# Three sets of small GpSimd loads beside a stream of large loads: attention over a cached window and a gated MLP for one token

## Chip, cores and metric

The kernel runs on one core of a Trainium2 chip. The metric is the device time of one execution in microseconds (us). The profile is of one execution on the chip, taken by the hardware profiler.

## What is computed

One token `x` (576 numbers, bfloat16) is normalised once and goes through two branches, whose results are added to `x`. Cut to what matters:

```python
def reference(A_x, A_k_cache, A_v_cache, A_wq, A_wo, B_x, B_w_in, B_w_sp, B_b_sp, B_w_out):
    def _A_ref(x, k_cache, v_cache, wq, wo):        # 32 query heads, 16 key heads of 128, window 4096
        q = (x @ wq).reshape(B, Sq, Hq, Dh) ...
        k = jnp.repeat(k_cache[:, :, Sk - W:, :], rep, axis=1)
        v = jnp.repeat(v_cache[:, :, Sk - W:, :], rep, axis=1)
        scores = jnp.einsum('bhqd,bhkd->bhqk', q, k) * Dh ** (-0.5)
        o = jnp.einsum('bhqk,bhkd->bhqd', _softmax(scores), v)
        return o... @ wo
    def _B_ref(x, w_in, w_sp, b_sp, w_out):
        z = _gelu(jnp.einsum('bsd,df->bsf', x, w_in))
        z1, z2 = z[..., :Fh], _layernorm(z[..., Fh:])
        g = jnp.einsum('ts,bsf->btf', w_sp, z2) + b_sp[None, :, None]
        return jnp.einsum('bsf,fd->bsd', z1 * g, w_out)
    xn = _layernorm(A_x)
    return A_x + _A_ref(xn, A_k_cache, A_v_cache, A_wq, A_wo) + _B_ref(xn, B_w_in, B_w_sp, B_b_sp, B_w_out)
```

The keys and values of the window are 16 heads x 4,096 positions x 128 numbers each; together with the weights 51 MB are read.

## The kernel before

The 16 key heads are worked on in four batches `b` of four. For each batch, `turn(b)` transposes the keys on VectorE in eight pieces (L209), `scores(b)` multiplies them with the query on TensorE (L254) and makes the softmax's exponentials (ScalarE, L274), and `values(b)` multiplies these with the values (L288) and sums up (L296). The calls stand in the order turn 0, scores 0, turn 1, scores 1, values 0, turn 2, scores 2, values 1, turn 3, scores 3, then `z_all` (the product with `w_in`, L311) and `gate` of the MLP branch, then values 2 and 3. At the end `row_of` (L376) adds the products with `wo` and `w_out` into one row, which is stored in two halves (L390 on SyncE, L391 on ScalarE). The schedule is manual: each engine runs its instructions in the order in which they are written, and a framework puts in the waits.

All large loads are issued by SyncE, in this order: `wq` in two cuts, k0, k1, v0, k2, v1, k3, `win`, v2, v3, `wo` in two cuts, `wout` in four (helpers `load`, L92, and `load_kv`, L98). Each has 128 rows, one for each partition. The tiles come from two pools of two buffers each, so a load waits until its buffer is free. In the pool `large` (20,736 numbers per partition) the tiles follow each other as wq, v0, v1, win, v3, wo: `wq`, `v1` and `v3` share one buffer, `v0`, `win` and `wo` the other. A tile of keys or values uses 16,384 of the 20,736 numbers (`NU * DH`), and `wo` uses 18,432 (`WR * D`). So `win` can be loaded once values(0) is done with v0, `v3` once values(1) is done with v1, and `wo` once z is done with `win`. SyncE's queue is in order: what stands behind a waiting load waits as well.

ScalarE issues five small loads at the start: `x_row` in three parts (L76) and the two numbers of `ws2` (L78, L79). GpSimd writes some constants at the start (up to `perm`, L147) and has nothing to do after that.

Of the kernel before, what the change touches and what calls it, by code (L numbers as in the profile page):

```python
# [15 lines left out]
D = 576  # L16
HQ = 32
HKV = 16
DH = 128
# [6 lines left out]
NU = W // NJ  # L26
# [7 lines left out]
WR = HQ * DH // P  # L34
# [8 lines left out]
def kernel(  # L43
# [14 lines left out]
    nc = tc.nc  # L58
# [24 lines left out]
    def unit(name, width):  # L83
        pool = small if width == SMALL else large
        return pool.tile([P, width], BF16, name=name, tag="u")
# [15 lines left out]
    kn, vn = {}, {}  # L101
# [14 lines left out]
    wo_t = unit("wo", LARGE)  # L116
# [28 lines left out]
    nc.gpsimd.tensor_copy(rep4[:], ident[:].rearrange("p (g q) -> p g q", g=4).unsqueeze(2).to_broadcast([P, 4, 4, 32]))  # L145
    perm = const.tile([P, 32, 4], BF16, name="perm")
    nc.gpsimd.tensor_copy(perm[:], ident[:].rearrange("p (q h) -> p h q", q=4))  # L147


    twice = const.tile([64, P], BF16, name="twice")  # L150
# [270 lines left out]
```

## Time and profile before

| what | before |
|---|---|
| median of 2 runs | 127.5 us (127.49 to 127.51) |
| profiled execution, its own time | 127.53 us |
| span of its instructions | 125.7 us |
| busy: TensorE matmul, VectorE, ScalarE, GpSimd | 78.6, 64.3, 10.2, 3.9 us |
| loads | 50.96 MB, 2,467 packets, 405 GB/s over the span |
| mean granted TensorE clock | 0.81 |

The span runs from the first to the last instruction. DMA queues are numbered: q1 is SyncE's, q10 ScalarE's, and each is spread over 16 DMA engines. A packet is one contiguous piece (here mostly one row of a load in one partition); a load ends with packets of 4 bytes that count it as done. A "releaser" is what ended a wait.

### The profile page before, as it was taken

What the parts mean: (1) busy time and instruction counts of PE and PEld (TensorE: products, weight loads), DVE (VectorE), ACT (ScalarE), POOL (GpSimd) and SP (SyncE); (2) the same over time, 40 slices, a digit from 0 to 9 for tenths busy, and PEclk for the clock granted to TensorE, in tenths of its full rate; (3) what the DMA queues carried; (4) which work ended last, traced back from release to release, by engine and by line L of the source; (5) the groups of instructions that cost most, each with busy time, mean ns of one, the idle gap of its engine ahead of it and who ended that gap; (6) DMA issues with size and microseconds to landing.
All of it is one profiled execution on the core that took longest, in us unless ns stands there. A gap on an engine that the chain in (4) does not pass through costs nothing.

```text
span 125.7 us, 1318 instructions
## 1 busy us (share of the span) xinstructions
PE 78.6 (62%) x534; PEld 37.6 (30%) x534; DVE 64.3 (51%) x129; ACT 10.2 (8%) x19; POOL 3.9 (3%) x10
## 2 busy tenths in 40 slices
PE   0042750099823998297599646699375097969861
PEld 0032220034211333145234223234063044435540
DVE  6315233499839995330999451999444830010001
ACT  2101000000030000301000031000120011010001
POOL 8400000000000000000000000000000000000000
PEclk9999998559996589755559999689976855595899
DMA  4999899998999989899898999999899999999950
GB/s 102 515 420 438 382 480 438 396 490 365 480 427 394 480 365 490 386 448 469 375 480 386 497 422 422 414 397 480 386 459 443 386 432 442 393 430 411 411 207 0
DMA packets 2467, 51.03 MB, mean 406 GB/s; under 512 B 284, under 2 KB 414, under 8 KB 670
## 3 DMA queue, kind: packets, MB, share of 16 engines
q1 hardware_dynamic: 2450, 50.96, 95.0%
q8 instruction: 4, 0.07, 0.2%
q14 instruction: 1, 0.01, 0.0%
q10 hardware_dynamic: 12, 0.00, 0.0%
HBM read 50.96 MB, written 0.00 MB: 405 GB/s over the span
## 4 chain that ended last, share of the span: by engine, by line
PE 43%; DMA 37%; DVE 10%; ACT 5%; SPq 2%; issue 1%; ACTq 0%
PE s L254 30%; DMA wout<-in_B_w_out_dram 19%; DMA k<-in_A_k_cache_dram 18%; PE pv L288 4%; ACT p L274 4%; DVE kt L209 4%; PE z L311 3%; PE op L296 2%; DVE sm L257 2%; PE tr L265 2%; SPq L92 2%; PE fin L376 1%; PE su L278 1%; DVE pt L276 1%; DVE m L267 1%
## 5 line engine op out<-in xcount | busy, mean ns | idle before, releaser
L254 PE MATMUL s<-kt,zq 128*128 128x512 bf16 x128 | 37.2, 456 | 11.1 <-DVE kt L209 11.1
L209 DVE STREAM_TRANSPOSE kt<-k 128x1024 f32<-128x1024 f32 x32 | 36.4, 1205 | 3.9 <-DMA k<-in_A_k_cache_dram 3.9
L254 PEld LDWEIGHTS <-zq 128*128 128x128 bf16 x128 | 14.4, 112 | 32.8 <-issue 22.1
L288 PE MATMUL pv<-v,pt 128*32 128x512 bf16 x128 | 12.4, 557 | 0.0
L274 ACT ACTIVATE p<-sm,nm 128x1024 bf16<-128x1024 f32 x4 | 4.6, 1147 | 67.9 <-DVE nm L270 67.9
L299 DVE TENSOR_TENSOR o_t<-op,rm 128x8 bf16<-128x8 f32 x4 | 0.7, 166 | 17.2 <-PE op L296 17.2
L276 DVE STREAM_TRANSPOSE pt<-p 128x1024 bf16<-128x1024 bf16 x4 | 5.0, 1245 | 5.4 <-ACT p L274 5.4
L296 PE MATMUL op<-selu,pvs 128*128 128x8 f32 x32 | 5.9, 311 | 2.9 <-ACT pvs L293 2.9
L257 DVE CUSTOM_DVE_ANT_1 sm<-s,cm 128x512 f32<-128x512 f32 x8 | 5.4, 671 | 3.7 <-PE s L254 3.7
L296 PEld LDWEIGHTS op<-selu,pvs 128*128 128x128 f32 x32 | 5.5, 259 | 5.8 <-ACT pvs L293 5.8
L278 PE MATMUL su<-sel,l 128*128 128x8 f32 x8 | 1.8, 293 | 7.6 <-ACT p L274 7.6
L218 PE MATMUL q_ps<-wq,xw 128*32 128x512 bf16 x36 | 4.2, 626 | 3.0 <-DVE xw L187 2.4
L376 PE MATMUL fin<-wo,o_p 128*1 128x288 bf16 x64 | 5.8, 357 | 0.1
L156 PE MATMUL x_ps<-one_bf,x_row 1*64 1x1 bf16 x9 | 1.2, 248 | 7.4 <-DMA x_row<-in_A_x_dram 7.4
L288 PEld LDWEIGHTS <-pt 128*32 128x32 bf16 x128 | 4.0, 128 | 5.6 <-issue 4.8
L388 DVE CAST res<-fin 1x288 bf16<-1x288 f32 x1 | 0.4, 446 | 9.9 <-PE fin L376 9.9
L265 PE MATMUL tr<-ident_f,m 128*128 128x128 f32 x8 | 1.9, 326 | 3.9 <-DVE m L263 3.9
L376 PEld LDWEIGHTS <-o_p 128*1 128x1 bf16 x64 | 3.4, 103 | 2.3 <-DVE o_p L370 0.3
L278 PEld LDWEIGHTS su<-sel,l 128*128 128x128 f32 x8 | 1.4, 218 | 8.4 <-ACT p L274 8.4
L311 PE MATMUL z<-win,xw 128*32 128x288 bf16 x72 | 3.8, 392 | 0.0
L376 PE MATMUL fin<-wout,hv 128*1 128x288 bf16 x36 | 2.6, 285 | 1.5 <-DMA wout<-in_B_w_out_dram 1.5
L293 ACT COPY pvs<-pv 128x512 f32<-128x512 f32 x4 | 2.3, 585 | 14.3 <-PE pv L288 14.3
(88 smaller groups left out, 39.0 us busy)
## 6 DMA issues: line engine op xcount, KB each, us to landing
k<-in_A_k_cache_dram SPq DMA_DIRECT2D x4, 4096.0 KB
v<-in_A_v_cache_dram SPq DMA_DIRECT2D x4, 4096.0 KB, 39.0
win<-in_B_w_in_dram SPq DMA_DIRECT2D x1, 5184.0 KB
wq<-in_A_wq_dram SPq DMA_DIRECT2D x1, 3584.0 KB
wo<-in_A_wo_dram SPq DMA_DIRECT2D x1, 2880.0 KB
wo<-in_A_wo_dram SPq DMA_DIRECT2D x1, 1728.0 KB, 20.0
wout<-in_B_w_out_dram SPq DMA_DIRECT2D x1, 1296.0 KB
wq<-in_A_wq_dram SPq DMA_DIRECT2D x1, 1024.0 KB, 4.9
```

Of the source, the lines that this page charges most:

```text
L209: nc.vector.transpose(t[:].rearrange("p c n e -> p (c n e)").bitcast(FP32), kn[b][:, UK * DH * k:UK * DH * (k + 1)].bitcast(FP32).rearrang ...
L218: nc.tensor.matmul(q_ps[32 * g:32 * g + 32, :], lhsT=xw[:, r, :], rhs=wq_t[:, 2048 * r + 512 * g:2048 * r + 512 * (g + 1)], start=r == 0, ...
L254: nc.tensor.matmul(s_ps[:], lhsT=zq[:, b, ce, ZPAD - 8 * k4:ZPAD - 8 * k4 + P], rhs=kt[b, 4 * kk + k4][:, c, :, e], start=k4 == 0 and ce = ...
L257: nc.vector.tensor_tensor_reduce(out=sm[:, kk, :].rearrange("p (n s) -> p n s", s=HB), in0=s_ps[:].rearrange("p (n s) -> p n s", s=HB), in ...
L265: nc.tensor.matmul(tr[:], lhsT=m1[:].to_broadcast([P, P]), rhs=ident_f[:], start=True, stop=True)
L274: nc.scalar.activation(p[:], sm[:].rearrange("p k n -> p (k n)"), ACT.Exp, bias=nm[:], accum_out=l[:])
L276: nc.vector.transpose(p_t[b][:].rearrange("p k u m -> p (k u m)"), p[:])
L278: nc.tensor.matmul(su[:], lhsT=l[:].to_broadcast([P, P]), rhs=sel8[:], start=True, stop=True)
L288: nc.tensor.matmul(pv[32 * g:32 * g + 32, :].rearrange("p (n d) -> p n d", n=4), lhsT=p_t[b][:, kk, u, :], rhs=v4[:, kk, u, :, :], start=k ...
L296: nc.tensor.matmul(op[:], lhsT=pvs[:, DH * u:DH * (u + 1)], rhs=selu[:, 8 * u:8 * u + 8], start=u == 0, stop=u == 3)
L311: nc.tensor.matmul(zp[i][32 * g:32 * g + 32, :], lhsT=xw[:, r, :], rhs=win_t[:, FH * r + a:FH * r + a + HW], start=r == 0, stop=r == NR - ...
L376: nc.tensor.matmul(fin[g][32 * g:32 * g + 1, :], lhsT=col, rhs=w[:, HW * g:HW * (g + 1)], start=start, stop=stop, tile_position=(0, 32 * g))
```

## The change

After the constants, GpSimd issues three sets of 16 loads. Their source is the first 34 rows of `w_out`, taken as 17 rows in two parts; load `i` of a set takes `n = 32 + 4 * i` numbers of each row and part, so 34 pieces of 64 to 184 bytes. They are written to partitions 0 to 16 of three tiles, `vn[0]`, `vn[3]` and `wo`, behind the columns that the kernel uses. Nothing reads them.

```diff
     perm = const.tile([P, 32, 4], BF16, name="perm")
     nc.gpsimd.tensor_copy(perm[:], ident[:].rearrange("p (q h) -> p h q", q=4))
+
+
+    few = B_w_out[0:34, :].rearrange("(m i) n -> i m n", m=2)
+    for t, first in ((vn[0], NU * DH), (vn[3], NU * DH), (wo_t, WR * D)):
+        a = first
+        for i in range(16):
+            n = 32 + 4 * i
+            nc.gpsimd.dma_start(t[0:17, a:a + 2 * n].rearrange("i (m c) -> i m c", m=2), few[:, :, 0:n])
+            a += 2 * n
```

In the built program GpSimd's queue has these 48 loads behind the copy to `perm`, and the other engines have the instructions they had. New waits: each GpSimd load from the ninth on waits for the one eight before it; the first of the second and of the third set wait for the tile's buffer to be free; SyncE waits for all 16 loads of the first set before it issues `win`, which takes v0's buffer; and SyncE's wait at the program's end takes in all GpSimd loads.

## The prediction

> **What bounds the kernel now.** I read the clock and span first (one core, span 125.7 us, granted clock 0.81), then the busy times by stretch, cut where the loads change.
>
> ```profile
> core 0: us, PE busy (x) PEld busy (x) DVE busy (x) ACT busy (x) POOL busy (x), PEclk, DMA share, GB/s
> 0.00:23.50 23.50, 6.53 (x53) 3.57 (x54) 8.46 (x31) 1.78 (x3) 3.93 (x10) 0.95 0.96 402
> 23.50:71.40 47.90, 35.64 (x144) 14.62 (x143) 35.03 (x48) 3.06 (x5) 0.00 (x0) 0.74 0.99 427
> 71.40:96.10 24.70, 17.35 (x152) 8.93 (x152) 14.50 (x27) 3.07 (x5) 0.00 (x0) 0.87 1.01 436
> 96.10:122.40 26.30, 18.28 (x177) 10.20 (x179) 5.86 (x23) 1.90 (x5) 0.00 (x0) 0.73 0.94 395
> 122.40:125.70 3.30, 0.77 (x12) 0.33 (x6) 0.45 (x1) 0.39 (x1) 0.00 (x0) 1.00 0.00 0
> ```
>
> The last three columns are clock, share of the 16 DMA engines and rate. The bulk loads run as one stream without a hole up to 122.4 us, and then 3.3 us are left for the last matmuls and the output. So the chip is bound by the stream; compute keeps up with it. A delay counts only if it makes a hole in the stream, adds to it, or ends after it. The chain of waits says the same at its end (start, length, what):
>
> ```profile
> 92.33 3.81 PE z L311 x72
> ...
> 97.48 24.29 DMA wout<-in_B_w_out_dram
> 121.78 0.04 issue
> 121.82 1.39 PE fin L376 x18
> ```
>
> Next, when SyncE issues the loads that come late, and when GpSimd is through (timeline):
>
> ```profile
> 4.14 0.39 POOL L147 COPY perm<-ident 128x128 bf16<-128x128 bf16 x1
> ...
> 57.38 0.34 SPq L92 DMA_DIRECT2D win<-in_B_w_in_dram  x1
> 69.17 7.79 SPq L98 DMA_DIRECT2D v<-in_A_v_cache_dram  x2
> 96.15 0.81 SPq L92 DMA_DIRECT2D wo<-in_A_wo_dram  x2
> ```
>
> `win` is issued at 57.4. What stands ahead of it (wq 4.7 MB, four k and two v of 4.19 MB: 29.9 MB) is moved by 23.5 x 402 + 47.9 x 427 = 29.9 MB, so at 71.4 us. `win` thus has 14 us to spare: it may be issued up to about 70 without a hole.
>
> Last, how a small load fares beside the stream. ScalarE's five small loads (x_row, ws2) are queue q10; here are the queues in the stretch from 5.8 to 11.2 us:
>
> ```profile
> q1 hardware_dynamic: 82, 2.35, 100.8%
> q10 hardware_dynamic: 6, 0.00, 0.1%
> ```
>
> 82 bulk packets (the 28,672-byte rows of wq) in 5.4 us x 16 engines x 1.008 are 1.06 us each. The six small ones start, by the packet records, at 5.82, 6.90, 7.96, 9.03, 10.09 and 11.16: one small packet, one bulk packet, in turn. Even the 4-byte completion of a load waits for a bulk packet after its data.
>
> **The change, part by part.** 48 loads on GpSimd's queue, 34 pieces of 64 to 184 bytes each: 1,632 pieces, 0.2 MB. Nothing is removed; compute order is unchanged. In the built program: a load waits for the eighth before it; set 1 waits for nothing; SyncE's `win` waits for all 16 of set 1; set 2 (vn[3]'s buffer) waits for the last matmul of values(1), 76.4 us; set 3 (wo's buffer) for the last of z, 96.1; and the wait at the program's end is for all 48. No matmul waits for any. SyncE's v2, v3, wo and wout are queued behind `win`; GpSimd has nothing else queued.
>
> *Bytes.* By the packet records a packet of 2 to 88 bytes holds its engine 9 ns, one of 384 bytes 21, one of 576 bytes 27. I take 12 ns: 1,632 x 12 / 16 = 1.2 us on each engine; with completions on all 16 engines 48 x 9 ns = 0.4 more. Bounds 0.9 to 2.9 us. Two thirds, 1.1 us, fall into the stream. A gain is excluded here: nothing leaves a stream that is already at a share of 0.99 to 1.01.
>
> *GpSimd's own time for a load.* No row shows one. Nearest are a load's issue on ScalarE and SyncE (0.21 to 0.54 us) and, as the engine's longest instruction, its memset of 2.12 us. Between 0.5 and 2.1 I take the geometric middle, 1.0 us. The Trainium skill (DMA: Bandwidth & Descriptors, Latency and other measured facts) has about 1 us to the first byte on GpSimd's path; no run here shows it, and by it the sum would stay.
>
> *Turns.* I take GpSimd's queue to be served as q10 is: one small piece, then one bulk packet. A row of k or v is 32,768 bytes: 16 x 32,768 / 427 GB/s = 1.23 us. If all 34 pieces lie on one engine, a load takes 35 packets x 1.2 = 42 us; if 17 rows go over nine engines, four pieces and a completion each, then 6 us, but eight loads stand in line in the same queue, 48 us. Both spreads give one rate: eight loads per 42 to 48 us.
>
> *Set 1.* First eight issued 5.5 to 13, done 48 to 55. The second eight would need until 91 to 98, but SyncE holds `win`, so the stream runs dry at about 72 (71.4 plus 0.5 for the new packets). Then small pieces flow alone: some 15 to 25 per engine at 10 to 30 ns, and 0.5 us to be seen (x_row's last packet 6.90, first matmul 7.38). `win` is issued at about 73.5; its first packet comes 0.9 us later (x_row: issue 0.73, packet 1.62): a hole of 2.5 us, bounds 1.5 to 6. `win` then lands at about 88, z still starts at 92.3 after scores(3), and wo is issued as before. The stream's end moves to 122.4 + 2.5 + 1.1 = 126.0, and the output to 129.3.
>
> *Set 2.* Opens at 76.4. From there 35 turns pass win's 8 packets (41,472 bytes, 1.52 us), v2's and v3's 16 (1.23) and 11 of wo's (23,040 to 13,824 bytes, 0.86 to 0.52): 12 + 20 + 8 = 40 us. First eight done 117 to 125; the second eight run among wout's short packets and end with the stream, about 127.5.
>
> *Set 3.* Its loads can be issued only then: 16 x 1.0 us, and 1 us to land: 144.5 us of span, which replaces 129.3 as the end. With 0.5 us a load it is 136.5, with 2.1 it is 162.
>
> The profiled execution took 127.53 us for a span of 125.7, 1.8 outside it; the median of the runs is 127.5. So 144.5 + 1.8 = 146 us.
>
> **The rivals.** *A: a whole load's share is one turn.* Each load then waits for one bulk packet per engine, 1.2 us, and the rate is GpSimd's, 1.0 us each: set 1 done by 5 + 16 + 4 = 25, long before 57; set 2 by 97; set 3 by 97 + 19 = 116, inside the span. What is left is the bytes: 127.5 + 1.2 to 1.6 = 129, not slower by 2%. It decides where the 32 loads of sets 2 and 3 fit between 76.4 and 125.7: at 1.5 us each, turns and issue together. The Trainium skill (DMA: Bandwidth & Descriptors, Queues, rings and completion order) speaks for it: the engine changes queues only at the end of a packet, which typically holds 9 to 17 descriptors. Against it are q10's rows, where a load's two descriptors are parted by a bulk packet; but q10 is ScalarE's queue, and GpSimd's isn't in this trace. Chance 0.27.
>
> *B: turns are cheap, but GpSimd is slow at writing the pieces.* With A's turns the end is 76.4 + 32 loads + 2 us; it passes 125.7 from 1.5 us a load on, and at 2.1 it is 146, so 148 us. For it: 34 pieces per load are made by software; against: all ten GpSimd instructions of the trace took 3.9 us together. Chance 0.13.
>
> *C: faster.* It would need a shorter stream, and nothing of it goes; 0.02 for what I don't see. That the loads are dropped because nobody reads them is excluded: they stand in the built program with their waits.
>
> **How the numbers follow.** Forecast 0.58, A 0.27, B 0.13, C 0.02. About 2% is what can be told from no change here. The forecast and B are slower: 0.71; A is within 2%: 0.27; faster 0.02. The time is 146. The range must take in A, since 0.27 is more than may be left out: from 127.8 (A with half of its packets hidden in the 3.3 us after the stream and small gaps) to 160 (1.7 us a load); above it lie slower GpSimd times, some 0.1. The slower cases alone: 138 to 160.
>
> **What would show it.** Pieces of 64 to 184 bytes with starts a bulk packet apart on an engine; SyncE's wait at `win` ended by GpSimd's loads at over 70 us instead of by PE at 57.4; a dent in the DMA row at 72 to 76; the second half of set 1 landing only in that dent; after the stream's end at 126 some 16 us in which only GpSimd's queue moves, and the last wait of SyncE ended by it. For A: `win` issued at 57.4, set 3 over before 122. For B: the same early `win`, but GpSimd's loads 1.5 us apart or more and a tail of them. Wrong altogether would be a stream that slows throughout (rate under 400 GB/s between 23.5 and 71.4): then the small pieces cost their engines much more than 12 ns each.

## The result and the profile after

The changed kernel takes 143.35 us (143.27 to 143.43, 2 runs) against 127.5: the ratio is 1.124, 95% interval 1.1195 to 1.1291. The profiled execution took 143.43 us for a span of 141.6. All times are medians of fast runs; one slow run, 135.4 us in the run of 16 rows in one part, is left out. The forecast said 146; the experiments below show that the sum came out near for a wrong reason.

The busy times by stretch, as before (last three columns: TensorE clock, share of the 16 DMA engines, GB/s):

```profile
core 0: us, PE busy (x) PEld busy (x) DVE busy (x) ACT busy (x) POOL busy (x), PEclk, DMA share, GB/s
0.00:23.50 23.50, 6.53 (x53) 3.60 (x54) 8.54 (x31) 1.78 (x3) 16.37 (x23) 0.97 0.94 358
23.50:71.40 47.90, 33.39 (x144) 13.34 (x143) 34.56 (x48) 3.07 (x5) 2.87 (x3) 0.80 1.01 404
71.40:96.10 24.70, 16.49 (x140) 8.66 (x144) 15.08 (x27) 3.07 (x5) 11.43 (x12) 0.88 1.00 400
96.10:122.40 26.30, 10.80 (x105) 5.43 (x97) 5.88 (x23) 1.90 (x5) 8.60 (x9) 0.69 1.00 374
122.40:141.60 19.20, 10.18 (x100) 5.37 (x99) 0.45 (x1) 0.39 (x1) 10.48 (x11) 0.68 0.74 203
```

The DMA engines are as full as before (0.94, 1.01, 1.00, 1.00), but move less: 358, 404, 400 and 374 GB/s where it was 402, 427, 436 and 395. So there is no hole; the stream itself runs slower, wherever GpSimd's loads are under way, and it ends at 137.57 us by the packet records instead of 122.43. That is 15.1 of the 15.9 us lost. The rest is after it: 4.1 us instead of 3.3, the last 18 matmuls at 2.4 us instead of 1.4.

The timeline has when GpSimd and SyncE issue (start, length, what):

```profile
4.48 7.73 POOL L155 DMA_DIRECT2D v<-in_B_w_out_dram  x8
12.71 0.95 POOL L155 DMA_DIRECT2D v<-in_B_w_out_dram  x1 [0.50 <-DMA v<-in_B_w_out_dram]
15.35 0.95 POOL L155 DMA_DIRECT2D v<-in_B_w_out_dram  x1 [1.68 <-DMA v<-in_B_w_out_dram]
...
59.91 0.33 SPq L92 DMA_DIRECT2D win<-in_B_w_in_dram  x1
...
77.18 7.61 POOL L155 DMA_DIRECT2D v<-in_B_w_out_dram  x8 [46.83 <-PE pv L297]
...
108.75 0.95 POOL L155 DMA_DIRECT2D wo<-in_B_w_out_dram  x1 [3.25 <-DMA v<-in_B_w_out_dram]
...
133.67 2.85 POOL L155 DMA_DIRECT2D wo<-in_B_w_out_dram  x3 [0.22 <-issue]
```

A load costs GpSimd 0.95 us. `win` is issued at 59.9, 2.5 us later than before and long before the stream would run dry. Of these 2.5 us set 1 accounts for 0.9: values(0) was done at 59.0, the last packet of set 1 came at 59.3. Set 3 starts at 108.75, as the loads of set 2 land one by one. GpSimd's last loads go out while the stream still runs; their last packet is at 138.2, and the end is again the chain through `wout`, the last matmuls and the output (chain of waits; start, length, what):

```profile
98.58 38.05 DMA wout<-in_B_w_out_dram
136.63 0.04 issue
136.68 2.37 PE fin L385 x18
139.04 0.43 DVE res L397
```

Where the DMA engines' time went is in the page's third part (packets, MB, share of 16 engines' span). Before:

```profile
q1 hardware_dynamic: 2450, 50.96, 95.0%
```

After:

```profile
q1 hardware_dynamic: 2450, 50.96, 92.8%
q0 software_dynamic: 1920, 0.30, 2.7%
```

GpSimd's queue is q0. Unlike the packets of the other queues, one of its packets can hold many pieces. Its packets hold each engine for 0.027 x 141.6 = 3.8 us. The same 2,450 bulk packets took 0.950 x 125.7 = 119.4 us of each engine before and take 0.928 x 141.6 = 131.4 now: 12.0 us more. The two make 15.8 us, the loss. And 0.30 MB is more than the loads carry: 48 loads are 0.202 MB, with 768 completions of 4 bytes 0.205. The packet records have the rest. They don't name the engine, but they have the queue, time and size of each packet. Each load has its data, in the first load of a set one packet of 2,176 bytes (34 x 64), and 15 times 136 bytes, 34 x 4, beside it. 48 x 15 x 136 bytes are the missing 0.098 MB. A load of more than about 4 KB is cut in two, and what stands beside it is cut in the same way: the last load of a set has packets of 4,232 and 2,024 bytes (23 and 11 pieces) and 15 times 92 and 44 bytes, 23 x 4 and 11 x 4. So there are 15 fillers of 4 bytes for each piece. That they lie on the 15 other engines is seen between 33.1 and 33.9 us: there the packets of one load (its data, 12 packets of 31 fillers, and the other three engines' last 3 fillers) are each followed by a bulk packet of its own, and these 16 run side by side.

The price can be read there too. In before, a bulk packet of a row of k or v takes 1.21 us. In the changed kernel the one that starts as a packet of fillers ends (paired by time, less than 10 ns apart) takes longer: by 0.02 us behind 2 fillers, 0.11 behind 11, 0.21 behind 23 and 0.28 behind 34 (medians; the last of 111 pairs). That is 8 to 10 ns for each filler, on each engine. The 34 fillers themselves are booked with 46 ns together.

So the theory that I tested: a load of 17 rows in two parts can't be dealt out to the engines. One engine gets all 34 pieces, and the 15 others get 34 fillers of 4 bytes. I call every piece, filler or completion that an engine passes a descriptor. With the completion every engine passes 35 descriptors for each load, 48 x 35 = 1,680, and 15.1 us / 1,680 = 9.0 ns each; most of it is booked on the bulk packets right behind. Rivals: a price for each load (L), for the bytes in small pieces (B; not the forecast's rival B), or for each real piece (P).

### The profile page after: what moved, and what is told of

Same layout as the page of the kernel before. It is cut to its first block, busy times and chain, and to the rows that moved or that the text cites. A ratio compares the mean times of both kernels' runs of the same rounds, so it can differ in the third digit from the quotient of the medians.

```text
span 141.6 us, 1378 instructions
## 1 busy us (share of the span) xinstructions
PE 77.4 (55%) x534; PEld 36.4 (26%) x534; DVE 64.5 (46%) x129; ACT 10.2 (7%) x19; POOL 49.7 (35%) x58
## 3 DMA queue, kind: packets, MB, share of 16 engines
q1 hardware_dynamic: 2450, 50.96, 92.8%
## 4 chain that ended last, share of the span: by engine, by line
DMA 64%; PE 18%; DVE 11%; ACT 2%; SPq 1%; issue 1%; ACTq 0%
DMA k<-in_A_k_cache_dram 37%; DMA wout<-in_B_w_out_dram 27%; PE s L263 13%; DVE kt L218 8%; PE z L320 3%; ACT p L283 2%; PE fin L385 2%; SPq L92 1%; DVE sm L266 1%; DVE pt L285 1%; PE tr L274 1%; DVE m L276 0%; DVE res L397 0%; PE su L287 0%; DVE m L272 0%
## 5 line engine op out<-in xcount | busy, mean ns | idle before, releaser
L155 POOL DMA_DIRECT2D v<-in_B_w_out_dram x32 | 30.6, 958 | 70.4 <-PE pv L297 46.8
L263 PE MATMUL s<-kt,zq 128*128 128x512 bf16 x128 | 36.3, 446 | 13.1 <-DVE kt L218 13.0
L155 POOL DMA_DIRECT2D wo<-in_B_w_out_dram x16 | 15.3, 954 | 15.8 <-DMA v<-in_B_w_out_dram 14.8
L297 PE MATMUL pv<-v,pt 128*32 128x512 bf16 x128 | 11.8, 537 | 7.4 <-DMA v<-in_A_v_cache_dram 7.4
L385 PE MATMUL fin<-wo,o_p 128*1 128x288 bf16 x64 | 6.6, 384 | 2.7 <-DMA wo<-in_A_wo_dram 2.7
L385 PE MATMUL fin<-wout,hv 128*1 128x288 bf16 x36 | 3.6, 363 | 5.3 <-DMA wout<-in_B_w_out_dram 5.3
L305 PE MATMUL op<-selu,pvs 128*128 128x8 f32 x32 | 4.2, 259 | 2.9 <-ACT pvs L302 2.9
L305 PEld LDWEIGHTS op<-selu,pvs 128*128 128x128 f32 x32 | 3.9, 191 | 5.5 <-ACT pvs L302 5.5
## 6 DMA issues: line engine op xcount, KB each, us to landing
v<-in_A_v_cache_dram SPq DMA_DIRECT2D x4, 4096.0 KB, 43.5
```

What stands on the lines that cost most here:

```text
L155: nc.gpsimd.dma_start(t[0:17, a:a + 2 * n].rearrange("i (m c) -> i m c", m=2), few[:, :, 0:n])
L263: nc.tensor.matmul(s_ps[:], lhsT=zq[:, b, ce, ZPAD - 8 * k4:ZPAD - 8 * k4 + P], rhs=kt[b, 4 * kk + k4][:, c, :, e], start=k4 == 0 and ce = ...
L297: nc.tensor.matmul(pv[32 * g:32 * g + 32, :].rearrange("p (n d) -> p n d", n=4), lhsT=p_t[b][:, kk, u, :], rhs=v4[:, kk, u, :, :], start=k ...
L305: nc.tensor.matmul(op[:], lhsT=pvs[:, DH * u:DH * (u + 1)], rhs=selu[:, 8 * u:8 * u + 8], start=u == 0, stop=u == 3)
L385: nc.tensor.matmul(fin[g][32 * g:32 * g + 1, :], lhsT=col, rhs=w[:, HW * g:HW * (g + 1)], start=start, stop=stop, tile_position=(0, 32 * g))
```

## The experiments

Each diff is against the changed kernel, cut to what matters; what is left out or moved are only the loads that nothing reads. Under each stands what I expected before the run. Where the text says how many engines have data or fillers, it takes the 16 packets of a load to lie on 16 engines.

**16 rows instead of 17.**

```diff
-    few = B_w_out[0:34, :].rearrange("(m i) n -> i m n", m=2)
+    few = B_w_out[0:32, :].rearrange("(m i) n -> i m n", m=2)
...
-            nc.gpsimd.dma_start(t[0:17, a:a + 2 * n]...
+            nc.gpsimd.dma_start(t[0:16, a:a + 2 * n]...
```

> The 48 loads take 16 rows in two parts instead of 17 (1,536 pieces instead of 1,632, 6% fewer bytes; nothing reads them). My theory after the changed kernel's trace: a load whose 17 rows can't be dealt out evenly puts 34 pieces on one engine and 34 fillers of 4 bytes on each of the other 15, so that every engine passes 34 + 1 descriptors for each load, at 15.1 us / (48 x 35) = 9.0 ns each. With 16 rows each engine gets one row, two pieces: 48 x 3 x 9 ns = 1.3 us, so 128.8 us, and GpSimd's queue shows 48 x (16 + 16) = 1,536 packets with no filler bytes (0.19 MB). Rival L (a price for each load, 15.1 / 48 = 0.315 us, whatever is in it): 143. Rival B (the bytes come slowly in small pieces): 142.4. Rival P (each real piece costs its engine 16 x 9 = 148 ns): 142.4.

Measured: 132.6 us, ratio 1.040 (1.035 to 1.044). Its page, third part:

```profile
q0 software_dynamic: 1536, 0.19, 1.0%
```

No filler bytes are left, and of 15.9 us lost 10.8 are gone with one row less. L, B and P fall. But 5.1 us is more than the 1.3 expected: the count is not all.

**34 rows in one part:** the same pieces and bytes.

```diff
-    few = B_w_out[0:34, :].rearrange("(m i) n -> i m n", m=2)
+    few = B_w_out[0:34, :]
...
-            nc.gpsimd.dma_start(t[0:17, a:a + 2 * n].rearrange("i (m c) -> i m c", m=2), few[:, :, 0:n])
-            a += 2 * n
+            nc.gpsimd.dma_start(t[0:34, a:a + n], few[:, 0:n])
+            a += n
```

> The same 34 pieces and the same bytes for each load, but as 34 rows in one part to 34 partitions. If the pieces are dealt out over the largest number of engines up to 16 that divides the rows, 34 rows go to 2 engines, 17 each, and the fillers on the others are 17: my theory gives 48 x 18 x 9 ns = 7.8 us, so 135.3 us, half of the loss. If instead two or three rows go to each engine: 129. Rivals L, B and P: 143, since the number of loads, the bytes and the pieces are the same.

Measured: 129.94 us, 1.020 (1.018 to 1.023). The packet records have three rows on each of 11 engines, one on a twelfth, and fillers of 12 bytes (3 x 4) elsewhere: the "two or three rows" case. The same 1,632 pieces and 0.2 MB cost 2.4 us instead of 15.9, so it is how they are dealt out that costs.

**Pieces of 8 bytes.**

```diff
-            n = 32 + 4 * i
+            n = 4
```

> Every piece is 8 bytes (4 numbers) instead of 64 to 184; 17 rows in two parts and 48 loads as in the changed kernel. My theory counts descriptors and not bytes: 143 us, at least 141, the fillers in the trace as before. Rival B: 15.1 x 8 / 124 = 1.0 us is left, 128.5. L and P: 143.

Measured: 143.81 us, 1.128 (1.126 to 1.130), no less than with fifteen times the bytes. In its queue

```profile
q0 software_dynamic: 1536, 0.11, 1.9%
```

nearly everything is filler: 48 x 15 x 136 bytes are 0.098 of the 0.11 MB. B is out.

**Four parts of half the width:** twice the pieces, the same bytes.

```diff
-    few = B_w_out[0:34, :].rearrange("(m i) n -> i m n", m=2)
+    few = B_w_out[0:68, :].rearrange("(m i) n -> i m n", m=4)
...
-            n = 32 + 4 * i
-            nc.gpsimd.dma_start(t[0:17, a:a + 2 * n].rearrange("i (m c) -> i m c", m=2), few[:, :, 0:n])
-            a += 2 * n
+            n = 16 + 2 * i
+            nc.gpsimd.dma_start(t[0:17, a:a + 4 * n].rearrange("i (m c) -> i m c", m=4), few[:, :, 0:n])
+            a += 4 * n
```

> Each load takes 17 rows in four parts of half the width: the same bytes, 68 pieces for each load instead of 34. My theory: 69 descriptors on every engine for each load, 48 x 69 x 9 ns = 29.8 us, so 157 us, and fillers of 68 x 4 = 272 bytes. Rivals L and B: 143. P: 158.

Measured: 159.41 us, 1.250 (1.248 to 1.252): 31.9 us lost for 15.9.

```profile
q0 software_dynamic: 2304, 0.40, 5.8%
```

0.40 MB are 0.205 and 48 x 15 x 272 bytes (68 x 4) of fillers. The stream ends 28.0 us later. By the records the last 4.5 of the 48 loads pass only after it, so it is 9.3 ns for each of 43.5 x 69 descriptors, and a bulk packet behind 64 fillers takes 0.54 us longer. The other 4 us are a tail: GpSimd's last packet is at 156.0, 5.5 us after the last bulk packet, and the span is 157.8. Here, not in the changed kernel, GpSimd's loads end last.

**17 rows in one part of double width.**

```diff
-    few = B_w_out[0:34, :].rearrange("(m i) n -> i m n", m=2)
+    few = B_w_out[0:17, :]
...
-            nc.gpsimd.dma_start(t[0:17, a:a + 2 * n].rearrange("i (m c) -> i m c", m=2), few[:, :, 0:n])
+            nc.gpsimd.dma_start(t[0:17, a:a + 2 * n], few[:, 0:2 * n])
```

> 17 rows in one part of double width: the same 48 loads and bytes, 17 pieces for each load instead of 34. My theory (34 + 1 descriptors on every engine for each load of the changed kernel, 9.0 ns each; the run with 68 pieces lost 31.9 us, about double): 17 + 1 descriptors, 48 x 18 x 9 = 7.8 us, 135.3 us, fillers of 17 x 4 = 68 bytes. A price for a load that can't be dealt out, whatever it holds: 143.

Measured: 130.37 us, 1.021 (1.017 to 1.025), a miss: I had taken 17 rows for what can't be dealt out. The packet records have two rows on eight engines, one on a ninth, and 8 bytes (2 x 4) of fillers on the other seven: three descriptors at most on each engine with the completion, not 18. With two or four parts 17 rows go to one engine, in one part to nine.

**16 rows to partitions 0, 8, 16 ... 120.**

```diff
-            nc.gpsimd.dma_start(t[0:17, a:a + 2 * n]...
+            nc.gpsimd.dma_start(t[0:128:8, a:a + 2 * n]...
```

(with `few` as for 16 rows)

> The loads of 16 rows in two parts again, but to partitions 0, 8, 16 ... 120 instead of 0 to 15. To partitions 0 to 15 they cost 5.1 us where three descriptors of 9 ns on each engine would be 1.3; the loads of 34 rows to 34 partitions cost 2.4, by count 1.7. If all engines writing into the same few partitions is what the rest is: 128.9 to 129.5 us here. If it has to do with two parts for a row, or with something else: 132.6 as before.

Measured: 139.82 us, 1.096 (1.092 to 1.099), which neither said. The step over partitions brought a wait that I had not meant: set 1 now waits for v0 itself to land (and set 2 for v3), and so `win` for set 1. Of this run the timeline, SyncE's waits (in total, times, longest) and a stretch:

```profile
45.08 4.09 POOL L155 DMA_DIRECT2D v<-in_B_w_out_dram  x8 [40.54 <-DMA v<-in_A_v_cache_dram]
```

```profile
75.36 0.33 SPq L92 DMA_DIRECT2D win<-in_B_w_in_dram  x1
...
129.37 0.31 SPq L399 DMA_DIRECT2D out_dram<-res  x1
```

```profile
SPq L92 <- DMA v<-in_B_w_out_dram: 26.0, 1, 26.0
...
SPq L425 <- DMA wo<-in_B_w_out_dram: 4.9, 1, 4.9
```

```profile
71.40:96.10 24.70, 16.73 (x150) 8.65 (x150) 16.02 (x25) 2.35 (x5) 0.00 (x0) 0.86 0.84 348
```

It tells nothing clean of the partitions, but it shows what my forecast described. `win` is issued at 75.4; the stream is dry from 73.9 to 76.3 (DMA share 0.84); and set 3 goes out last: its last packet is at 134.2, SyncE's last wait is for it (4.9 us), and the span ends 8.7 us after the output is issued (2.1 in the changed kernel). Hole and tail are real things, at loads that wait longer than those of the changed kernel.

**Only the first set.**

```diff
-    for t, first in ((vn[0], NU * DH), (vn[3], NU * DH), (wo_t, WR * D)):
+    for t, first in ((vn[0], NU * DH),):
```

> Only the first of the three sets, 16 loads. My theory: the loss goes with the number of descriptors on the engines, so a third of it: 16 x 35 x 9 ns = 5.0 us, 132.5 us; the stream slow up to about 35 us and at its old rate after, win issued 5 us or less later than before and with no hole at it. By the forecast on record (small pieces in single turns, win held back until the stream is dry) win would be issued at over 70 us and the loss be 2.5 to 4 us: 130 to 131.5, with a hole at 72.

Measured: 133.25 us, 1.043 (1.040 to 1.047): 5.6 us, 0.35 for each load, where 48 loads lost 0.33 each. Its stretches:

```profile
23.50:71.40 47.90, 33.49 (x133) 13.79 (x133) 32.92 (x45) 3.07 (x5) 2.86 (x3) 0.70 1.01 404
71.40:96.10 24.70, 16.72 (x112) 7.74 (x114) 16.16 (x29) 3.07 (x5) 0.00 (x0) 0.93 1.00 430
```

The rate is 404 GB/s while the set is under way (last packet at 59.4, not 35 as I expected) and 430 after it; `win` is issued at 60.6. No hole.

**One load from ScalarE, none from GpSimd.**

```diff
-    for t, first in ((vn[0], NU * DH), (vn[3], NU * DH), (wo_t, WR * D)):
+    for t, first in ((vn[0], NU * DH),):
...
-        for i in range(16):
+        for i in range(1):
-            nc.gpsimd.dma_start(
+            nc.scalar.dma_start(
```

> One load of 17 rows in two parts, issued by ScalarE instead of GpSimd (in place of all 48). If ScalarE's queue is served one piece at a time and GpSimd's a whole load at a time: 34 pieces in q10, one for each bulk packet, from about 11 (behind the two numbers of ws2) to about 50 us, and no fillers, so q10 has 12 + 34 + 1 = 47 packets; the time within 0.5 us of before, 127.5. If ScalarE's is served by the load as well: its pieces within 2 us.

Measured: 127.59 us, ratio 1.000 (0.997 to 1.002). DMA queues from 12.4 to 48.9 us:

```profile
q1 hardware_dynamic: 545, 15.74, 100.1%
q10 hardware_dynamic: 34, 0.00, 0.1%
```

The page counts 47 packets in q10, so 34 pieces and no fillers. They take 36 us, 1.22 us apart but for four that follow the one before at once: one piece for each bulk packet. So the turns that I saw in q10 and gave to GpSimd's queue are ScalarE's own. GpSimd's first load, 34 pieces of 64 bytes as well, is one packet record of 2,176 bytes and 88 ns.

**18 rows in two parts** (`few` of 36 rows, `t[0:18, ...]`).

> 18 rows in two parts, 36 pieces for each load. So far 17 rows in two parts went to one engine with 34 fillers on each other; 17 rows in one part went two rows to an engine. If the pieces of a two-part load are dealt out over the largest number of engines up to 16 that divides the rows, it is 9 engines with 4 pieces each and 4 fillers elsewhere: 48 x 5 x 9 ns = 2.2 us and the some 40 to 70 ns for each load that the well dealt runs had on top of that (1.9 to 3.4 us): 131 to 133 us. If any number of rows that isn't a multiple of 16 goes to one engine: 48 x 37 x 9 = 16.0 us, 144.

Measured: 131.93 us, 1.034 (1.029 to 1.038). The records have four pieces on each of nine engines and 16 bytes (4 x 4) on the other seven. One row more than the changed kernel's, and 11.4 us less.

**16 rows in one part** (as the run of 17 rows in one part, with 16).

> 16 rows in one part of double width to partitions 0 to 15: one piece on each engine for each load. The run of 16 rows in two parts lost 5.1 us, 3.8 more than its three descriptors at 9 ns; 17 rows in one part, to nearly the same partitions, 2.7. If the rest goes with the pieces written into the same 16 partitions (32 there, 16 here): about half of it, 130 us. If it goes with the load alone (0.1 us each): 132. If it is the two parts: 128.9.

Measured: 133.15 us, 1.042 (1.036 to 1.047; single runs 132.0 to 133.6). Half the pieces cost no less than 16 rows in two parts. Of the three, only the price for each load, about 0.1 us, stands, and for loads of 16 rows alone: 17 and 34 rows in one part lose 0.05 to 0.06 us a load in all.

**The changed kernel's loads at other partitions** (`t[96:113, ...]`).

> The loads of the changed kernel, 17 rows in two parts, to partitions 96 to 112 instead of 0 to 16. My theory has the loss in the number of descriptors on each engine, whatever they write to: 143 to 144 us. If it is a crowd at partitions 0 to 16 (which bulk rows, or the descriptors themselves, share): at least 3 us less, under 140.

Measured: 143.11 us, 1.121 (1.119 to 1.124). At partitions 96 to 112 the loads cost what they cost at 0 to 16.

**16 rows in two parts at other partitions** (`t[96:112, ...]`).

> 16 rows in two parts to partitions 96 to 111 instead of 0 to 15. If the 3.8 us that the well dealt loads cost over 1.3 come from 16 engines writing into 16 neighbouring partitions: 132.6 again. If from those partitions, 0 to 15, in particular: 129 to 129.5.

Measured: 132.04 us, 1.034 (1.031 to 1.038), nearer to 132.6 than to 129: it isn't partitions 0 to 15 in particular. All loads together:

| rows x parts | descriptors of each engine for a load | lost, us | stream ends later, us |
|---|---|---|---|
| 17 x 4 | 69 | 31.9 | 28.0 |
| 17 x 2 (changed kernel; at 96) | 35 | 15.9; 15.5 | 15.1; 14.8 |
| 17 x 2, 8 bytes each | 35 | 16.3 | 15.4 |
| 18 x 2 | 5 | 4.3 | 4.0 |
| 34 x 1 | 4 | 2.4 | 2.1 |
| 17 x 1 | 3 | 2.7 | 2.7 |
| 16 x 2 (at 96) | 3 | 5.1 (4.4) | 4.9 (4.5) |
| 16 x 1 | 2 | 5.5 | 4.9 |

With 69 descriptors the count at 9 ns explains 27.0 of the 28.0 us that the stream loses, and with 35 and pieces of 8 bytes 15.1 of 15.4. For the loads of few descriptors it explains 0.9 to 2.2 us; what is left, 0.4 to 4.0 us, is not ordered by count. In the records it lies again on the bulk packets right behind: in the run of 16 rows in two parts, 0.03 to 0.14 us behind the two pieces of a load and 0.04 behind its completion, against 0.007 behind a completion in the changed kernel. Why loads of 16 rows lose more than those of 17 or 34 in one part stays open, and so does why a filler holds up the packet behind it.

## Why the forecast was near, and which steps of it failed

The kernel got slower, as forecast, and the time lies in the range; the sum behind it does not hold.

**The bound** was right: the stream sets the end, before and after, and nothing got faster.

**Bytes** is the step that failed in size, and it is the whole result: I priced a small packet at 12 ns, near the 9 ns measured for a descriptor, but counted 1,632 pieces over 16 engines, 102 for each, and 48 completions. Each engine passes 48 x 34 = 1,632 pieces or fillers, not 102. 1.1 us in the stream by the sum were 15.1. The price hardly shows in a filler's own record (34 of them are booked with 46 ns); it shows on the bulk packet behind. What I should have asked is what the engines get that have no piece of a load; q10's loads, with one packet on one engine and a completion, could not tell.

**GpSimd's own time**, 1.0 us from bounds far apart, was 0.95, which is luck: it is 0.5 to 0.6 for the well dealt loads and 1.06 with 68 pieces. The about 1 us to the first byte that the forecast quoted is not what the trace shows: the first packet of set 1 came 4.7 us after GpSimd began the load (4.48, 9.19), that of set 2 4.4 us after (77.18, 81.61), which may include a bulk packet's turn of 1.1 to 1.5 us.

**Turns** failed: GpSimd's queue is not served piece by piece. The scalar load shows that q10 is, so the row was read rightly and carried over wrongly. What a turn of GpSimd's queue holds is a packet: the records have up to 34 pieces in one, cut at about 4 KB, and 64 in the loads of four parts. The Trainium skill's rule that I weighed there (DMA: Bandwidth & Descriptors, Queues, rings and completion order: the engine drains a whole packet before it changes queues) agrees with GpSimd's queue. On ScalarE's each piece is a packet of its own, so the typical size that it gives does not hold there.

**Set 1 and the hole** fell with it: 8 loads of two turns (data, completion) and 8 of three are 40 turns, and from 9.2 to 59.3 us they took 1.25 us each, about one bulk packet. `win` went out at 59.9, not 73.5, with no hole instead of 2.5 us.

**Sets 2 and 3:** I let set 3 start only when set 2 was over, at 127.5. But each load waits only for the eighth before it, and the loads of set 2 landed one by one, so set 3 started at 108.75. It ended with the stream (138.2 against 137.6), so the tail of 15.2 us that made most of my sum did not exist. My terms 1.1, 2.5 and 15.2 became 15.1, 0 and 0. That 146 is near 143.35 is chance.

**Rival A** was right that a packet takes one turn, and that no long tail follows the stream. But a load took two or three turns one after another, 3.1 us in set 1, so the rate was not GpSimd's 1.0: set 1 was done at 59, not 25, and set 3 at 138, not 116. Its time, 129, was wrong because it took the same 1.2 to 1.6 us for the pieces. **Rival B** fell: 0.95 us is under its 1.5. The last paragraph of the forecast named a stream that slows throughout as the sign that all of it was wrong; 404 GB/s between 23.5 and 71.4 missed the 400 given there and meant just that.

On how rows are dealt out the Trainium skill has a rule that I did not weigh (DMA: Bandwidth & Descriptors, Why a DMA increments its semaphore by 16 and not by 1): a load runs on the largest number of engines up to 16 that divides its rows; some GpSimd loads are instead cut into sixteenths, rounded up. The runs agree: 17 rows in two parts went to one engine, 18 to nine, 16 to sixteen, and 17 and 34 rows in one part were cut by two and three. By its rule one engine would have had 34 pieces, the others no data; the fillers are what the runs add.

## What to carry to other kernels

A load issued by GpSimd can cost every DMA engine, not only those that carry its data. Count its descriptors for the engine with the most pieces, multiply by all loads and about 9 ns, and set that against the slack of the DMA stream. For loads that are dealt out this is too little: here they cost 0.05 to 0.11 us each. A row more or less, or the same pieces as one row each, took two thirds or more of the loss away. A full DMA share with a lower rate was the sign: something passed the engines that moves few bytes. And a forecast that lands near is no proof of its terms: each term has its own row to look at.

## What the hardware showed that I had not expected

- Fillers: GpSimd's queue gives each engine without data as many 4-byte descriptors as the most loaded engine has pieces (34, 68, 4, 3 and 2 in five shapes).
- The price of a filler is mostly booked on other work: q0's packets took 3.8 us of each engine, the unchanged bulk packets 12.0 us more, 8 to 10 ns on the packet right behind for each filler.
- The same 17 rows in two parts have no fillers in ScalarE's queue: 34 packets of 11 ns by the records, one after another in turn with the bulk packets.
- Writing to every eighth partition made the framework wait for the whole tile's load: 40.5 us of waiting for GpSimd and a hole in the stream.
